# Loading token blocks 12 to 15 in two halves and moving one key transpose (kt12) forward, in a one-core transformer layer

## The chip, the core and the metric

The kernel runs on one core of a Trainium2 chip. The core has five engines that run their own instruction streams and meet through semaphores: TensorE (PE; its weight loads are listed apart as PEld), VectorE (DVE), ScalarE (ACT), GpSimd (POOL) and SyncE (SP), which here does nothing but issue DMAs, one after another, in the order of its program. SBUF is the on-chip memory, PSUM holds the results of matmuls in 8 banks. The metric is the device time of one execution in microseconds (us); smaller is better.

## The reference

One pre-norm layer on x of 2048 tokens by 640 features, in bf16: a memory-augmented attention over 4 segments of 512 tokens (32 heads of 20 features), then a dense part with 1728 hidden features. Cut to what matters:

```python
q = (x @ wq) ...; k = (x @ wk) ...; v = (x @ wv) ...      # x is layernorm(A_x); heads of 20, 4 segments
phi = lambda t: jnp.where(t > 0, t + 1.0, jnp.exp(t))
for s in range(N):                                         # 4 segments in order
    logits = einsum('bhqd,bhkd->bhqk', qs, ks) * scale + mask
    a_dot = einsum('bhqk,bhkd->bhqd', softmax(logits), vs)
    pq = phi(qs)
    a_mem = einsum(pq, M) / (einsum(pq, z) + 1e-06)
    outs.append(g * a_mem + (1.0 - g) * a_dot)
    pk = phi(ks)
    M = M + einsum('bhld,bhle->bhde', pk, vs)
    z = z + einsum('bhld->bhd', pk)
...
h = x + attention(layernorm(x)) @ wo
h2 = h + silu(layernorm(h) @ w1) @ w2
```

## The kernel before

**Tiling.** A token block is 128 tokens on the 128 partitions, so there are 16 blocks, four to a segment. x_tok holds 12 blocks; blocks 12 to 15 use the places of blocks 0 to 3 again, once their results are stored. All weights stay in SBUF.

**Steps and their names.** The work is cut into tasks, and each task has a name that says step, segment and index:

- x12 loads token blocks from memory (line 578). `load_x(12, 4, ...)` loads four blocks, 12 to 15, in one DMA of 640 KB.
- n1_st, n1_r, n1_ap and n1_tr with a block's number are the first layer norm: statistics on DVE (line 742), the reciprocal root on POOL (lines 760 and 763), the normalisation on DVE into xn_rot (line 769), and a DMA transpose from SP into xT (line 798). n2_ with the same letters is the second layer norm; its transposes go into hT, by the same line 798.
- pr are the query and key projections on PE (line 866), qe their evacuation from PSUM; v are the value projections (line 827). pr220, the first key or query projection of segment 2, reads xT of all four blocks 8 to 11.
- vt copies parts of q and k within SBUF into QKV (line 914, twelve small DMAs in a segment); vp does this for phi(q) into phiQv (line 927).
- qk are attention scores on PE (line 964), e their exponentials on ACT (line 976), mk the causal masks on POOL (line 987), av the products with v (line 1008), tn and nm the transposition, the memory term and the division (lines 1038, 1042, 1056 to 1062), ad their sum (line 1070). The first five head groups of a segment read QK, the last three read QKV. qk13a0 belongs to group 5 of segment 1 and so is the first that needs that segment's QKV.
- phb is the last step of phi (line 902 for keys and queries alike). kt with a segment and an index is the DMA transpose of phi(k) of one chunk of heads (line 1207), kg and kh gather parts of it (line 1198), mz is the product phi(k)·v on PE (line 1225), ma adds it to the memory (line 1241), mb masks it (line 1249). kt12 is segment 1, chunk 2; mz10 needs kt12 and kt13.
- ot and wo are the transposes of the attention's output (line 1264) and its projection (line 1272), rs the first residual (line 1280).
- h1, th and s are the hidden layer: matmul on PE (line 1307), tanh on ACT (line 1316), their product on DVE (line 1322), which frees the PSUM bank. h2 is the second matmul (line 1349), o the second residual (line 1362), out the store of a block (line 1367).

**Order.** The order of all tasks is written out by hand in one long table, ORDER. Every engine runs its share of the table in that order. The name after a slash is the engine (S for SP, A for ACT, G for POOL, D for DVE), the numbers after a colon are the slots (PSUM banks, buffers) that the task takes. The semaphore waits are derived from what tasks read and write. So a DMA that waits on SP holds everything behind it on SP. The stores of a segment's four blocks share one counter; a load that uses their places again waits for those stores that stand ahead of it in the table.

**Interleaving.** The segments overlap: the dense part of one segment runs in PE's stream between the attention of the next.

Of the kernel before, what the change touches and what calls it, by code (L numbers as in the profile page):

```python
# [234 lines left out]
class Graph:  # L235
# [51 lines left out]
    def schedule(self):  # L287
# [37 lines left out]
D = 640  # L325
# [23 lines left out]
P = {"ln1": -5.0, "ln1s": 0.524, "v": -2.2, "vs": 0.4, "pr": -0.979, "prc": 0.831, "prw": 0.404, "phq": 0.3,  # L349
# [37 lines left out]
qk10a0:0 e10a+:4 w_w2_4 s0_9_0 n1_tr8:0 h1_0_13_0:7 th0_13_0:1 pha101:0 h2_0_0:4 h2_0_1 mm2 ma02/D:7,2,6,3 pha130:0  # L387
phb100 ot2 qk10b0:0 mk8b_384 n1_ap9:2 av8:6 n1_tr10 mzc2 pha110:0 mzc4 s0_13_0 pha131:1 vt12/S w_w2_5 ex131:1 mk9b_0
mk9b_384 e10b+:6 mk9a_0 av9:7 phb131 kt13:0 vt13/S mzc1 oe9/D:1 vt17/S ex130:1 mzc6 pha111:2 oe8/D:0 phb101 vt11/S
h2_0_2 ex110:0 vt18/S n1_tr9 qk10e0:0 e10e2:0 n1_tr11 mk10b_0 vt15/S mk10b_384 h2_0_3 e10e0 mk10e_0 ex121:2 h2_1_0:6  # L390
o0 qk11a0:2 e11a+:3 phb130 pha121:1 phb121 kt12:1 vt14/S wo3:0 phb110 rs3 n2_st3:2 h2_1_1 qk11b0:2 mb00:0,0 ex140:2
n2_r3/G tn8:0 nm8:1,1 phb140 vp111/S:0 e11b+:1 mk10e_256 vp14/S h2_1_2 h2_1_3 o1 qk12a0:2 mk10a_0 vp10/S wo2:0 rs2
av10:6 vp13/S mk11a_0 vp110/S vp16/A e12a+:5 n2_ap3:2 ex141:1 mk11b_0 qk12b0:2 mz10:0 mb01:0,0 e12b0:2 pr220:7
oe10/D:0 ma10 e12b2 qk13a0:0 kg12/G:0 mk12a_0 mk11b_384 qe220/D:0 tn9:4 nm9:2,0 ad9:0 v20:6 e13a+:4 n2_tr3 kh13/G
# [13 lines left out]
rs6 n2_st6:3 ex220:2 av16:0 oe16/D:1 wo7:6 rs7 n2_r6/D qk17a0:2 wo4:0 vt28/S e17a+:0 h1_0_9_1:7 th0_9_1:0 ex240:1  # L408
kg10/G vt27/S n2_st7:0 mk18b_384 vt21/S mk17b_384 vt211/S h1_0_3_1:6 mk17a_0 rs4 th0_3_1:1 n2_st4:2 s0_9_1 qk18e0:2
e18e0:1 n2_r4/D wo5:0 s0_3_1 vt23/S h1_0_2_1:7 e18e2 mk18e_0 phb240 rs5 th0_2_1:0 s0_2_1 h1_0_1_1:6 th0_1_1:1 vt24/S  # L410
s0_1_1 qk18a0:2 e18a0:2 vt25/S av17:1 oe17/A:0 kt23:1 h2_2_0:6 h2_2_1 n2_ap6:1 n2_st5:6 n2_tr6:0 n2_r7/G mk18e_256
n2_ap7:3 n2_tr7 phb220 vt22/S e18a2 qk19b0:0 pha230:0 phb230 vp21/S:0 e19b0:4 tn17:4 nm17:3,1 n2_ap4:1 n2_tr4 pha200:0
h2_2_2 e19b2 h2_2_3 mk18a_0 n2_r5/G qk19a0:0 h2_3_0:4 h2_3_1 e19a2:0 o2 ad17:0 vp22/S e19a0 n2_ap5:3 n2_tr5 out2/S
mk19a_0 vp24/S ex200:0 kh14/D av18:6 oe18/D:0 vt210/A phb200 qk20b0:0 e20b+:3 h2_3_2 mk19b_0 h2_3_3 o3 vp25/S ex201:1
kg14/G mz12:7 mb10:0,0 tn18:1 nm18:3,0 mk19b_384 av19:0 h1_1_10_0:6 oe19/A:0 phb201 qk21b0:0 th1_10_0:1 tn16:4 ma12
s1_10_0:0 nm16:0,1 e21b+:4 mk21b_0 mk21b_384 h1_1_7_0:7 h1_1_4_0:6 ad18 th1_7_0:1 th1_4_0:0 s1_7_0 s1_4_0 qk20a0:0
e20a+:2 out3/S x12/S n1_st12:6 n1_r12/G h1_1_1_0:4 th1_1_0:1 s1_1_0 vp210/S h1_1_12_0:7 th1_12_0:0 mk20b_0 n1_st13:0
n1_r13/G mk20b_384 vp28/S qk20e0:0 h1_1_11_0:5 n1_ap12:3 e20e+:0 h1_1_8_0:4 qk21a0:0 s1_12_0 th1_11_0:1 h1_1_5_0:6
e21a+:5 th1_5_0:0 n1_st15:5 mk21a_0 n1_ap13:2 mk20a_0 s1_11_0 s1_5_0 mk20e_0 mk20e_256 h1_1_2_0:7 th1_2_0:1 s1_2_0
# [43 lines left out]
def build(nc, es, A_x, A_wq, A_wk, A_wv, A_wo, A_beta, B_x, B_w1, B_w2, out):  # L463
# [10 lines left out]
    G = Graph(pools)  # L474
# [100 lines left out]
    def load_x(b0, n, prio, bw=2.1, kind="plain", engs=(SP, AC)):  # L575
        s0 = b0 % 12
        dma(f"x{b0}", [], [(X[b], [0]) for b in range(b0, b0 + n)],
            lambda e: e.dma_start(out=x_tok[:, s0:s0 + n, :], in_=xv[:, b0:b0 + n, :]), prio, bw, kind, engs=engs)
# [846 lines left out]
```

## Time and profile before

| | us |
|---|---|
| three runs | 297.81, 298.67, 298.39 |
| median | 298.39 |
| the profiled execution | 298.91 |
| its span in the trace | 297.1 |
| PE busy in the span | 285.1 (96%) |
| DVE busy | 223.2 (75%) |
| ACT busy | 217.6 (73%) |
| POOL busy | 141.1 (48%) |

The table says that PE is busy nearly all of the span. A busy share is an average over the whole span, however, and tells nothing of single waits; these are read from the chain of waits (the work that ended last, followed back from the end), from the timeline of each engine, where idle time ahead of a row stands in brackets with what ended it, and from the DMA view, which gives the time from a DMA's issue to its landing. Times in these views count from the start of the span. A row of SPq or ACTq is the issue of a DMA, not its transfer.

### The profile page before, as it was taken

Reading aid. Unit: us, or ns where it says so; the run is one execution under the profiler, and the core shown is the slowest. Engines: PE = TensorE matmul, PEld = TensorE weight load, DVE = VectorE, ACT = ScalarE, POOL = GpSimd, SP = SyncE. Lnnn points to the kernel's source line nnn. Section 1 sums busy time; section 2 is a strip of 40 time slices with the busy share of each in tenths; the row PEclk is TensorE's granted clock in tenths of the full one; section 3 lists DMA queues with packets and bytes.
Section 4 is the critical chain, followed back from the end, with each engine's and each line's share of the span. In section 5 each row is a group of like instructions: output and inputs, shape, how many; then the busy total and the mean of one; then the engine's idle time right before and its main releaser. Section 6 shows DMA issues by size and latency. Waiting matters only on the chain.

```text
span 297.1 us, 7435 instructions
## 1 busy us (share of the span) xinstructions
PE 285.1 (96%) x2989; PEld 167.8 (56%) x2989; DVE 223.2 (75%) x503; ACT 217.6 (73%) x263; POOL 141.1 (48%) x261
## 2 busy tenths in 40 slices
PE   8898889999998999999998999999999999999996
PEld 5675445556664456566643444455665457764575
DVE  5897988868887979899678967759967688626522
ACT  5857997999997999999788999788759751013400
POOL 6226964665446776646525656354576630200000
PEclk9999999999999999999999999999999999999999
DMA  7946773924473422153343400154071023230002
GB/s 232 369 124 99 175 132 99 254 73 125 82 87 64 60 67 38 29 107 73 66 141 65 82 4 2 26 80 84 16 105 32 0 56 78 67 68 24 23 22 90
DMA packets 49906, 25.40 MB, mean 85 GB/s; under 512 B 39488, under 2 KB 48032, under 8 KB 49872
## 3 DMA queue, kind: packets, MB, share of 16 engines
q1 hardware_dynamic: 47656, 22.55, 35.9%
q10 hardware_dynamic: 2216, 2.38, 2.6%
q8 instruction: 24, 0.39, 0.6%
q14 instruction: 10, 0.08, 0.1%
HBM read 10.41 MB, written 2.62 MB: 44 GB/s over the span
## 4 chain that ended last, share of the span: by engine, by line
PE 73%; DVE 8%; ACT 7%; DMA 7%; issue 1%; POOL 1%; ACTq 1%; SPq 1%; DVEq 0%
PE ps_all L1349 18%; PE ps_all L1307 15%; PE ps_all L866 10%; PE ps_all L1272 7%; PE ps_all L827 6%; ACT PT L976 6%; PE ps_all L964 6%; PE ps_all L1008 5%; DMA x_tok<-in_A_x_dram 4%; DMA phiKt<-phiK 2%; DVE stt L742 2%; PE ps_all L1038 1%; PE ps_all L1225 1%; PE ps_all L1042 1%; PE ps_all L1301 1%
## 5 line engine op out<-in xcount | busy, mean ns | idle before, releaser
L976 ACT ACTIVATE PT<-ps_all 128x1024 bf16<-128x1024 f32 (+1 forms) x118 | 152.9, 1328 | 19.9 <-PE ps_all L964 16.4
L987 POOL TENSOR_SCALAR_AFFINE_SELECT PT<-PT 128x512 bf16<-128x512 bf16 x128 | 81.8, 651 | 50.7 <-ACT PT L976 49.0
L1349 PE MATMUL ps_all<-w_sb,sT 128*128 128x320 bf16 (+2 forms) x462 | 64.9, 295 | 0.1
L1307 PE MATMUL ps_all<-hT,w_sb 128*128 128x512 bf16 (+1 forms) x325 | 62.8, 337 | 1.3 <-DVE sT L1322 1.2
L1316 ACT ACTIVATE th<-ps_all 128x512 f32<-128x512 f32 (+2 forms) x70 | 33.9, 503 | 35.1 <-PE ps_all L1307 30.5
L1349 PEld LDWEIGHTS ps_all<-w_sb,sT 128*128 128x128 bf16 x462 | 43.2, 98 | 18.4 <-issue 2.0
L1322 DVE SCALAR_TENSOR_TENSOR sT<-th,ps_all 128x512 bf16<-128x512 f32 (+2 forms) x70 | 37.9, 561 | 18.7 <-ACT th L1316 17.9
L1307 PEld LDWEIGHTS ps_all<-hT,w_sb 128*128 128x128 bf16 x325 | 29.8, 98 | 26.7 <-issue 3.4
L763 POOL TENSOR_TENSOR rst<-rst,eps_c 128x1 f32<-128x1 f32 x32 | 18.6, 584 | 27.6 <-DVE rst L757 26.2
L742 DVE BATCH_NORM_STATS2 stt<-x_tok 128x6 f32<-128x320 bf16 x62 | 27.2, 482 | 2.7 <-DMA x_tok<-in_A_x_dram 2.2
L1362 DVE SCALAR_TENSOR_TENSOR x_tok<-ps_all,x_tok 128x640 bf16<-128x640 f32 (+3 forms) x18 | 13.3, 744 | 17.1 <-PE ps_all L1349 17.1
L1070 POOL TENSOR_TENSOR otok<-on 128x320 bf16<-128x320 bf16 x24 | 19.2, 802 | 13.8 <-DVE on L1062 13.8
L1272 PE MATMUL ps_all<-wo_sb,oT 128*128 128x320 bf16 x160 | 23.7, 299 | 0.0
L883 DVE CAST QK<-ps_all 128x512 bf16<-128x512 f32 x25 | 17.2, 687 | 5.9 <-PE ps_all L866 5.8
L1062 DVE TENSOR_TENSOR on<-ps_all,rd 128x640 bf16<-128x640 f32 x24 | 19.8, 824 | 0.9
L1272 PEld LDWEIGHTS ps_all<-wo_sb,oT 128*128 128x128 bf16 x160 | 15.0, 98 | 7.2 <-issue 1.8
L866 PE MATMUL ps_all<-xT,wkr 128*128 128x512 bf16 x75 | 18.7, 380 | 0.0
L827 PE MATMUL ps_all<-wv_sb,xT 128*128 128x320 bf16 x120 | 18.3, 299 | 0.4
L866 PE MATMUL ps_all<-xT,wqr 128*128 128x512 bf16 x75 | 18.2, 380 | 0.0
L1008 PE MATMUL ps_all<-PT,Vx 128*32 128x512 bf16 (+3 forms) x384 | 16.4, 301 | 0.0
L769 DVE TENSOR_SCALAR xn_rot<-x_tok,mvt,rst 128x640 bf16<-128x640 bf16 x32 | 14.7, 470 | 1.4 <-POOL rst L763 1.2
L889 ACT ACTIVATE ex<-QK 128x512 bf16<-128x512 bf16 x25 | 15.5, 630 | 0.1
(106 smaller groups left out, 336.2 us busy)
## 6 DMA issues: line engine op xcount, KB each, us to landing
w_sb<-in_B_w_dram SPq DMA_DIRECT2D x5, 432.0 KB, 3.6
x_tok<-in_A_x_dram SPq DMA_DIRECT2D x3, 640.0 KB, 8.7
w_sb<-in_B_w_dram SPq DMA_DIRECT2D x3, 480.0 KB, 3.6
out_dram<-x_tok ACTq DMA_DIRECT2D x9, 160.0 KB, 1.8
out_dram<-x_tok SPq DMA_DIRECT2D x6, 160.0 KB, 2.0
QKV<-QK SPq DMA_DIRECT2D x12, 72.0 KB
wo_sb<-in_A_wo_dram SPq DMA_DIRECT2D x1, 800.0 KB, 10.6
w_sb<-in_B_w_dram SPq DMA_DIRECT2D x1, 640.0 KB, 5.3
```

Source lines behind the costliest of these rows:

```text
L742: T.add(DV, lambda e, hh=hh: e.bn_stats(out=stt[:, s, 6 * hh:6 * hh + 6], in_=xb[:, 320 * hh:320 * hh + 320]), reads=R((xa, xsub)), writes ...
L827: fns.append(lambda e, c=c, hh=hh: e.matmul(bank(ps, hh)[:, 0:320], lhsT=xT_[:, c, 128 * i:128 * i + 128], rhs=wv_sb[:, c, 320 * hh:320 * ...
L866: fns = [lambda e, kc=kc: e.matmul(bank(ps)[:, lo:hi], lhsT=wt[:, kc, c, :], rhs=xT_[:, kc, lo:hi], start=(kc == 0), stop=(kc == NC - 1)) ...
L976: T.add(AC, lambda e: e.activation(out=pt[:, pta.slot, q0:q0 + nq, 0:width], in_=sc3[:, b0:b0 + nq, 0:width], func=ACT.Exp, scale=SCALE), ...
L987: T.add(PO, lambda e: e.affine_select(out=v, in_=v, pattern=[[0, 4], [1, 128]], compare_op=ALU.is_ge, fill=0.0, base=0, channel_multiplier ...
L1008: fns.append(lambda e, j=j, r=r, h=h, pa=pa, pt=pt, co=co, q0=q0, ji=ji: e.matmul(bank(po)[32 * r:32 * r + 32, q0:hi], lhsT=Vx[:, vx.slot, ...
L1062: T.add(DV, lambda e: e.tensor_tensor(out=on[:, ona.slot, :, :].rearrange("p b (x e) -> p b x e", e=DH), in0=v[:, :, :, 0:DH], in1=r2.unsq ...
L1272: fns.append(lambda e, c=c, hh=hh: e.matmul(bank(ps, hh)[:, 0:320], lhsT=oT[:, c, 128 * i:128 * i + 128], rhs=wo_sb[:, c, 320 * hh:320 * h ...
L1307: fns = [lambda e, c=c: e.matmul(bank(ps)[:, lo:hi], lhsT=w1_sb[:, c, 128 * f:128 * f + 128], rhs=hT[:, c, lo:hi], start=(c == 0), stop=(c ...
L1316: T.add(AC, lambda e: e.activation(out=th[:, tha.slot, lo:hi], in_=bank(ps)[:, lo:hi], func=ACT.Tanh, scale=0.5), reads=R((ps, [0])), writ ...
L1322: T.add(DV, lambda e: e.scalar_tensor_tensor(out=sT[:, f, lo:hi], in0=th[:, tha.slot, lo:hi], scalar=1.0, in1=bank(ps)[:, lo:hi], op0=ALU. ...
L1349: fns.append(lambda e, f=f, t0=t0, fr=fr, hh=hh, n=n: e.matmul(bank(pa, hh)[:, 0:n], lhsT=sT[:, f, t0:t0 + 128], rhs=w2_sb[:, fr, c0 + 320 ...
```

## The change

Two things change. First, `load_x(12, 4, ...)` becomes two loads of two blocks (320 KB each), x12 and x14. x14 stands in the table where x12 stood, behind out3, the store of block 3; x12 now stands behind kt23. Second, kt12 stands ahead of n1_tr9 and n1_tr11 in place of behind n1_tr9, n1_tr11 and vt15. No arithmetic changes.

```diff
@@ ORDER @@
-h2_0_2 ex110:0 vt18/S n1_tr9 qk10e0:0 e10e2:0 n1_tr11 mk10b_0 vt15/S mk10b_384 h2_0_3 e10e0 mk10e_0 ex121:2 h2_1_0:6
-o0 qk11a0:2 e11a+:3 phb130 pha121:1 phb121 kt12:1 vt14/S wo3:0 phb110 rs3 n2_st3:2 h2_1_1 qk11b0:2 mb00:0,0 ex140:2
+h2_0_2 ex110:0 vt18/S qk10e0:0 e10e2:0 mk10b_0 mk10b_384 h2_0_3 e10e0 mk10e_0 ex121:2 h2_1_0:6 o0 qk11a0:2 e11a+:3
+phb130 pha121:1 phb121 kt12:1 n1_tr9 n1_tr11 vt15/S vt14/S wo3:0 phb110 rs3 n2_st3:2 h2_1_1 qk11b0:2 mb00:0,0 ex140:2
...
-s0_1_1 qk18a0:2 e18a0:2 vt25/S av17:1 oe17/A:0 kt23:1 h2_2_0:6 h2_2_1 n2_ap6:1 n2_st5:6 n2_tr6:0 n2_r7/G mk18e_256
+s0_1_1 qk18a0:2 e18a0:2 vt25/S av17:1 oe17/A:0 kt23:1 x12/S h2_2_0:6 h2_2_1 n2_ap6:1 n2_st5:6 n2_tr6:0 n2_r7/G
...
-e20a+:2 out3/S x12/S n1_st12:6 n1_r12/G h1_1_1_0:4 th1_1_0:1 s1_1_0 vp210/S h1_1_12_0:7 th1_12_0:0 mk20b_0 n1_st13:0
+qk20a0:0 e20a+:2 out3/S x14/S n1_st12:6 n1_r12/G h1_1_1_0:4 th1_1_0:1 s1_1_0 vp210/S h1_1_12_0:7 th1_12_0:0 mk20b_0
...
@@ build @@
         if s == NSEG - 1:
-            load_x(12, 4, 8 * s + P["x3"])
+            load_x(12, 2, 8 * s + P["x3"])
+            load_x(14, 2, 8 * s + P["x3"])
```

What moves is SP's stream. The first place is in segment 1, with the QKV copies of that segment around it; phiKt<-phiK is kt12, the two transposes into xT are n1_tr9 and n1_tr11, and the copies are vt17, vt11 and vt18 at the top, vt15 in the middle, vt14 at the bottom. What an instruction waits for stands in brackets.

```order
 L914 DMA QKV<-QK 8x2x1024 x2
 L914 DMA QKV<-QK 8x1x1024
+L1207 DMA_TRANSPOSE phiKt<-phiK 128x4x128 [waits s_dve]
 L798 DMA_TRANSPOSE xT<-xn_rot 128x5x128 x2
 L914 DMA QKV<-QK 8x1x1024
-L1207 DMA_TRANSPOSE phiKt<-phiK 128x4x128 [waits s_dve]
 L914 DMA QKV<-QK 8x2x1024
```

kt12, with its wait for DVE, moved past two transposes and a copy.

The second place is later on SP, in the tail of segment 1: phiKt<-phiK is kt23, the transposes into hT are those of blocks 6 and 7.

```order
 L914 DMA QKV<-QK 8x1x1024
 L1207 DMA_TRANSPOSE phiKt<-phiK 128x4x128 [waits s_pool,s_dve]
+L578 DMA x_tok<-in_A_x_dram 128x2x640 [waits l_out0]
 L798 DMA_TRANSPOSE hT<-xn_rot 128x5x128 [waits s_pe,s_dve]
 L798 DMA_TRANSPOSE hT<-xn_rot 128x5x128 [waits s_dve]
```

A load of two blocks is new here; it waits for the stores out0 and out1. Further on, behind out3, the load of four blocks has become one of two:

```order
 L1367 DMA out_dram<-x_tok 128x640 [waits s_dve]
-L578 DMA x_tok<-in_A_x_dram 128x4x640 [waits l_out0]
+L578 DMA x_tok<-in_A_x_dram 128x2x640 [waits l_out0]
 L927 DMA phiQv<-phiQ 8x1024
 L927 DMA phiQv<-phiQ 8x1x512
```

It waits for all four stores, as before. On DVE one wait is new: the statistics of block 15, the first reader of x14, wait for it. PE, ACT and POOL run the same instructions in the same order.

More of the change, by code (lines that the diff above doesn't have):

```diff
@@ L410 @@
 e18e0:1 n2_r4/D wo5:0 s0_3_1 vt23/S h1_0_2_1:7 e18e2 mk18e_0 phb240 rs5 th0_2_1:0 s0_2_1 h1_0_1_1:6 th0_1_1:1 vt24/S
-s0_1_1 qk18a0:2 e18a0:2 vt25/S av17:1 oe17/A:0 kt23:1 h2_2_0:6 h2_2_1 n2_ap6:1 n2_st5:6 n2_tr6:0 n2_r7/G mk18e_256
-n2_ap7:3 n2_tr7 phb220 vt22/S e18a2 qk19b0:0 pha230:0 phb230 vp21/S:0 e19b0:4 tn17:4 nm17:3,1 n2_ap4:1 n2_tr4 pha200:0
-h2_2_2 e19b2 h2_2_3 mk18a_0 n2_r5/G qk19a0:0 h2_3_0:4 h2_3_1 e19a2:0 o2 ad17:0 vp22/S e19a0 n2_ap5:3 n2_tr5 out2/S
-mk19a_0 vp24/S ex200:0 kh14/D av18:6 oe18/D:0 vt210/A phb200 qk20b0:0 e20b+:3 h2_3_2 mk19b_0 h2_3_3 o3 vp25/S ex201:1
@@ L415 @@
-kg14/G mz12:7 mb10:0,0 tn18:1 nm18:3,0 mk19b_384 av19:0 h1_1_10_0:6 oe19/A:0 phb201 qk21b0:0 th1_10_0:1 tn16:4 ma12
-s1_10_0:0 nm16:0,1 e21b+:4 mk21b_0 mk21b_384 h1_1_7_0:7 h1_1_4_0:6 ad18 th1_7_0:1 th1_4_0:0 s1_7_0 s1_4_0 qk20a0:0
-e20a+:2 out3/S x12/S n1_st12:6 n1_r12/G h1_1_1_0:4 th1_1_0:1 s1_1_0 vp210/S h1_1_12_0:7 th1_12_0:0 mk20b_0 n1_st13:0
-n1_r13/G mk20b_384 vp28/S qk20e0:0 h1_1_11_0:5 n1_ap12:3 e20e+:0 h1_1_8_0:4 qk21a0:0 s1_12_0 th1_11_0:1 h1_1_5_0:6
-e21a+:5 th1_5_0:0 n1_st15:5 mk21a_0 n1_ap13:2 mk20a_0 s1_11_0 s1_5_0 mk20e_0 mk20e_256 h1_1_2_0:7 th1_2_0:1 s1_2_0
@@ L420 @@
-vp20/S qk22a0:0 e22a0:6 kt20:0 vp211/S kg20/G:0 n1_st14:4 vp26/S th1_8_0:1 kg23/D n1_r14/D h1_1_6_0:5 th1_6_0:0 vp29/S
-n1_tr12:0 v30:6 n1_r15/D s1_6_0 e22a2 h1_1_0_0:0 n1_ap14:0 s1_8_0 n1_ap15:3 mk22a_0 kh23/G av21:1 ve30/A:1
+s0_1_1 qk18a0:2 e18a0:2 vt25/S av17:1 oe17/A:0 kt23:1 x12/S h2_2_0:6 h2_2_1 n2_ap6:1 n2_st5:6 n2_tr6:0 n2_r7/G
+mk18e_256 n2_ap7:3 n2_tr7 phb220 vt22/S e18a2 qk19b0:0 pha230:0 phb230 vp21/S:0 e19b0:4 tn17:4 nm17:3,1 n2_ap4:1
+n2_tr4 pha200:0 h2_2_2 e19b2 h2_2_3 mk18a_0 n2_r5/G qk19a0:0 h2_3_0:4 h2_3_1 e19a2:0 o2 ad17:0 vp22/S e19a0 n2_ap5:3
@@ new lines @@
+n2_tr5 out2/S mk19a_0 vp24/S ex200:0 kh14/D av18:6 oe18/D:0 vt210/A phb200 qk20b0:0 e20b+:3 h2_3_2 mk19b_0 h2_3_3 o3
+vp25/S ex201:1 kg14/G mz12:7 mb10:0,0 tn18:1 nm18:3,0 mk19b_384 av19:0 h1_1_10_0:6 oe19/A:0 phb201 qk21b0:0 th1_10_0:1
+tn16:4 ma12 s1_10_0:0 nm16:0,1 e21b+:4 mk21b_0 mk21b_384 h1_1_7_0:7 h1_1_4_0:6 ad18 th1_7_0:1 th1_4_0:0 s1_7_0 s1_4_0
+qk20a0:0 e20a+:2 out3/S x14/S n1_st12:6 n1_r12/G h1_1_1_0:4 th1_1_0:1 s1_1_0 vp210/S h1_1_12_0:7 th1_12_0:0 mk20b_0
+n1_st13:0 n1_r13/G mk20b_384 vp28/S qk20e0:0 h1_1_11_0:5 n1_ap12:3 e20e+:0 h1_1_8_0:4 qk21a0:0 s1_12_0 th1_11_0:1
@@ L422 @@
+h1_1_5_0:6 e21a+:5 th1_5_0:0 n1_st15:5 mk21a_0 n1_ap13:2 mk20a_0 s1_11_0 s1_5_0 mk20e_0 mk20e_256 h1_1_2_0:7 th1_2_0:1
+s1_2_0 vp20/S qk22a0:0 e22a0:6 kt20:0 vp211/S kg20/G:0 n1_st14:4 vp26/S th1_8_0:1 kg23/D n1_r14/D h1_1_6_0:5 th1_6_0:0
+vp29/S n1_tr12:0 v30:6 n1_r15/D s1_6_0 e22a2 h1_1_0_0:0 n1_ap14:0 s1_8_0 n1_ap15:3 mk22a_0 kh23/G av21:1 ve30/A:1
 mb12:0,0,0,0 av20:2 qk22b0:3 vp23/S th1_0_0:0 s1_0_0 n1_tr13 mz20:7 ma20 oe21/A:1 e22b+:1 mk22b_0 vp27/S tn21:0
```

## The prediction, made before the changed kernel was run

> **What bounds the kernel now.** I read the chain of waits first, over its whole length. Apart from the start it is TensorE (PE) work, one matmul group behind another, and outside that it holds few stretches in which a DMA sets the pace. Two of them concern what the diff touches. Columns: start in us, length in us, what.
>
> ```profile
> 91.27 2.43 DMA phiKt<-phiK
> ...
> 149.77 2.44 DMA out_dram<-x_tok
> 152.22 4.76 DMA x_tok<-in_A_x_dram
> 157.01 0.90 DVE stt L742 x2
> ```
>
> The first is kt12, which lands at 93.70; mz10, the product that needs it, starts then. The second is three long: store of block 3, load of blocks 12 to 15, and the statistics of block 12 (L742) that wait for it. Next the table of busy time by stretch (length, then busy time of PE, PEld, DVE, ACT, POOL, granted clock, DMA share, GB/s), to see whether time won at one place lasts.
>
> ```profile
> 94.00:120.00 26.00, 25.88 (x307) 14.08 (x303) 21.18 (x45) 23.70 (x28) 18.74 (x32) 1.00 0.28 50
> 175.00:200.00 25.00, 24.99 (x266) 12.56 (x265) 16.68 (x32) 21.58 (x25) 13.13 (x21) 1.00 0.22 31
> ```
>
> PE is busy 25.88 of 26.00 and 24.99 of 25.00 us at full clock, with ACT next. So behind both places the kernel runs on PE's sequence, and a microsecond that PE gains there should move everything behind it, as long as no SP transfer stands at a fixed time.
>
> **First part: kt12 ahead.** The engines' timelines around it; the bracket is idle time and what ended it.
>
> ```profile
> 85.85 0.64 DVE L902 TENSOR_TENSOR phiK<-phiK,ex 128x512 bf16<-128x512 bf16 x1
> 87.14 3.38 SPq L798 DMA_TRANSPOSE xT<-xn_rot  x2
> 90.56 0.66 SPq L914 DMA_DIRECT2D QKV<-QK  x1
> 92.51 0.72 SPq L914 DMA_DIRECT2D QKV<-QK  x1
> 92.54 0.40 PE L964 MATMUL ps_all<-QK 20*128 20x384 bf16 x8
> 93.75 0.47 PE L1225 MATMUL ps_all<-Vx,phiKt 128*128 128x84 bf16 x8 [0.81 <-DMA phiKt<-phiK]
> 94.06 1.24 PE L866 MATMUL ps_all<-xT,wqr 128*128 128x512 bf16 x5
> 95.24 0.39 PE L964 MATMUL ps_all<-QKV 20*128 20x512 bf16 x4
> ```
>
> SP issues without a pause here. kt12's own input (phb121, DVE L902) is ready at 85.85 + 0.64 = 86.49, but SP gets to it at 91.27, behind the two xT transposes and one QKV copy. In the changed order SP reaches kt12 at 87.14, after 86.49, so its wait for DVE costs SP nothing, and nothing that stands behind it is held for that reason. PE is free at 92.54 + 0.40 = 92.94; kt12 then has 5.8 us to land where the chain shows 2.43. The 0.81 us before mz10 go.
>
> What is late next? The two xT transposes n1_tr9 and n1_tr11 and one QKV copy (vt15) each go one kt12 later. The instructions are the same, so SP is back in step for the next QKV copy, vt14, at 92.51. The group behind mz10, pr220 (L866), needs xT of all four blocks, and PE would want it at 92.94 + 0.47 = 93.41. Time from issue to landing of n1_tr9, of n1_tr11, and of an xT transpose of segment 3 that follows no other transpose closely:
>
> ```profile
> xT<-xn_rot SPq DMA_TRANSPOSE x1, 4.2
> xT<-xn_rot SPq DMA_TRANSPOSE x1, 3.7
> xT<-xn_rot SPq DMA_TRANSPOSE x1, 2.6
> ```
>
> In their new place the two take SP from 87.14 + 1.24 = 88.4 to 91.75, if they need their 3.38 again (one of them was hindered: two hT transposes further on take 2.55, so 1.25 to 1.3 is the plain issue). If the last issue is plain, n1_tr11 begins at 91.75 - 1.25 = 90.5 and lands between 90.5 + 2.6 = 93.1 and 90.5 + 3.7 = 94.2. The first end is in time for 93.41; the last gives back all of the 0.81. If it is the hindered one, it begins earlier, at 89.6, and lands by 89.6 + 4.2 = 93.8. I take the first, the row of a transpose of the same size on a free queue, since the hindrance fell before 90.5.
>
> Behind pr220 PE has qk13a0 (95.24), the first matmul on the QKV copies of this segment; it needs all of them, vt14 last. That copy keeps its issue at 92.51. No row gives its landing; the table by quarter microseconds bounds it:
>
> ```profile
> 94.75:95.00 0.25, 0.25 (x3) 0.06 (x1) 0.00 (x0) 0.18 (x1) 0.25 (x1) 1.00 0.03 8
> 95.00:95.25 0.25, 0.25 (x6) 0.02 (x4) 0.00 (x0) 0.00 (x0) 0.25 (x1) 1.00 0.00 0
> ```
>
> DMA data (last column) runs out by 95.0, and 92.51 plus kt12's own 2.43 is 94.94. PE would be there at 95.24 - 0.81 = 94.43. So the QKV copy probably takes over as the wait, and qk13a0 starts near 94.95, which is 0.29 earlier than before. Some of the rest comes back at once, because the next PE groups do not need the copies but the evacuation of pr220, which is 0.8 earlier. Bounds of the first part: 0 (nothing, or a few hundredths lost) to 0.81 won; between 0.29 and 0.81 I take 0.4, nearer to the copy.
>
> **Second part: the load in halves.** The later half, x14, stays where the whole load stood, behind the store of block 3. The first half, x12, goes behind kt23.
>
> ```profile
> 128.78 0.59 SPq L1367 DMA_DIRECT2D out_dram<-x_tok  x1
> ...
> 135.48 1.23 SPq L1207 DMA_TRANSPOSE phiKt<-phiK  x1
> 138.05 2.55 SPq L798 DMA_TRANSPOSE hT<-xn_rot  x2
> ...
> 152.22 0.41 SPq L578 DMA_DIRECT2D x_tok<-in_A_x_dram  x1
> ```
>
> x12 waits only for the stores of blocks 0 and 1. The second of these is issued at 128.78 and by the 2.44 of block 3's store lands at 131.2, so the wait is over when SP comes to it at 135.48 + 1.23 = 136.71. Its issue (0.41 for the whole load) fits before 138.05, when DVE releases the next transpose: it costs SP nothing. If that cover were gone, 0.4 us of SP would be added. It lands before 136.71 + 4.76 = 141.5, the time of a load twice its size, 13 us ahead of need.
>
> ```profile
> 155.71 1.09 ACT L1316 ACTIVATE th<-ps_all 128x512 f32<-128x512 f32 x2
> 156.66 1.91 ACT L976 ACTIVATE PT<-ps_all 128x2048 bf16<-128x2048 f32 x1
> 153.44 1.33 DVE L1322 SCALAR_TENSOR_TENSOR sT<-th,ps_all 128x512 bf16<-128x512 f32 x2 [0.22 <-ACT th L1316]
> 157.01 0.89 DVE L742 BATCH_NORM_STATS2 stt<-x_tok 128x6 f32<-128x320 bf16 x2 [2.23 <-DMA x_tok<-in_A_x_dram]
> 160.55 0.88 DVE L742 BATCH_NORM_STATS2 stt<-x_tok 128x6 f32<-128x320 bf16 x2
> 156.28 1.25 PE L1307 MATMUL ps_all<-hT,w_sb 128*128 128x512 bf16 x5
> 158.75 1.25 PE L1307 MATMUL ps_all<-hT,w_sb 128*128 128x512 bf16 x5 [1.22 <-DVE sT L1322]
> 159.93 0.40 PE L964 MATMUL ps_all<-QKV 20*128 20x512 bf16 x4
> ```
>
> DVE stands 2.23 us for the load. Queued behind it is the s step (L1322) that frees the PSUM bank PE wants at 157.53; PE stands 1.22 for that. With x12 there, DVE does the statistics at 154.8. The s step then waits only for its tanh on ACT, the first of the pair that begins at 155.71, so it ends near 156.9, before PE asks. PE's 1.22 go. Not 2.23: two groups on, PE's scores (159.93) need the banks that ACT's exponential frees at 156.66 + 1.91 = 158.57, so PE cannot gain more than 159.93 - 158.6 = 1.33. I take 1.2, the idle time itself.
>
> x14 is issued at 152.22 as before and needs at most the whole load's 4.76: 157.0. Its first reader, the statistics of block 15, came 160.55 - 157.01 = 3.5 us behind those of block 12, so now at 154.8 + 3.5 = 158.3. Hidden by 1.3 us.
>
> **Sum.** 0.4 + 1.2 = 1.6 us. The profiled execution took 298.91, of which 297.1 are the span and 1.8 lie around it: 295.5 and 297.3. The median of the runs lies 0.52 below the profiled one, so 298.39 - 1.6 = 296.8.
>
> **The rivals.** *The first part gives nothing*: the xT transpose of block 11 lands at 94.2, not 93.1, and PE starts pr220 when it did before. For it: in the old order it took 3.7. Against it: a transpose behind a quiet queue took 2.6. Only 1.2 remain: 297.2.
>
> *The second wait is replaced*: everything comes earlier by DVE's order, but ACT, which works through 155.71 to 158.57 without a gap, keeps PE waiting for scores, and half of the 1.2 goes. With 0.4 from the first part: 1.0 gained at most, or 0.6 if the xT transpose is late too, so 297.4 to 297.8. If the early half is for some reason held by its wait until the old place, only the first 0.4 is left: 298.0.
>
> *Slower*: the early half is put ahead of the four hT transposes of segment 1, and stretches them. The copy ahead of their later two, these two, and PE's first group on them:
>
> ```profile
> 141.37 0.66 SPq L927 DMA_DIRECT2D phiQv<-phiQ  x1
> 142.40 2.56 SPq L798 DMA_TRANSPOSE hT<-xn_rot  x1
> 145.71 1.97 SPq L798 DMA_TRANSPOSE hT<-xn_rot  x1
> ...
> hT<-xn_rot SPq DMA_TRANSPOSE x1, 3.4
> 149.27 1.25 PE L1307 MATMUL ps_all<-hT,w_sb 128*128 128x512 bf16 x5
> ```
>
> The last lands at 145.71 + 3.4 = 149.1, and PE uses it at 149.27: almost no slack. An issue took 2.56 instead of 2.55 / 2 = 1.28 when it was hindered. Should x12's data hinder the two transposes at 138.05 so, SP would be 2 x 1.28 = 2.6 behind, less the 0.4 that it idles before 142.40: the last would land at 151.3. PE, 0.4 early at 148.9, would wait 2.4, and after the 1.2 won later the kernel would be 2.4 - 1.6 = 0.8 slower: 299.2, more if the later two are hindered further. It decides once SP is over 1.4 us behind at 142.40 (0.2 + 1.4 = the 1.6 won). Against it: x12 is over by 141.5, and DVE, not SP, released 138.05.
>
> The Trainium skill bears on this rival (DMA: Bandwidth & Descriptors, section Queues, rings and completion order): on each DMA engine the descriptors of one ring are consumed in the order of the ring, so the transposes behind x12 begin their data after it. By that alone the transpose at 138.05 is moved to 141.5 at the latest and the one at 145.71 not at all, so by the rule this case would be far less likely than I make it. The trace agrees only in part: the transposes of 4.2 and 3.7 stand behind a row of copies, but the one at 142.40, hindered too, stands behind a small one (141.37).
>
> **How the numbers follow.** Both parts as summed: 0.50 (own range 296.2 to 297.2, from 2.14 and 1.2 won). First part nothing: 0.20. Second replaced or held: 0.17. Slower: 0.13. No change here means within 0.3%, 0.9 us, about what a measurement of this kernel can tell. Faster by more needs under 297.5: the first two cases and a little of the third less the edges, 0.70. Same 0.17, slower 0.13. The range, 295.8 to 298.3, takes in the first three cases and leaves out the slower one and some scatter of the runs (0.86 us between the three shown).
>
> **What would show it.** The 0.81 before L1225 at 93.75 and the 2.23 before L742 are gone from the waits; pr220 does not wait for xT; the QKV matmul behind it waits a few tenths for a copy; x14's reader does not wait; PE is 0.4 early at 100 and 1.6 early from 165 to the end. It is wrong if the first L1307 group near 149 waits for an hT transpose, or if the lead at 165 is not there at 250.

## The result, and the profile after

The changed kernel took 297.28 us (median of 19 runs, 296.56 to 298.40), the kernel before in the same comparison 298.47 us (19 runs, 297.44 to 299.66). The ratio is 0.9962, 95% interval [0.9948, 0.9976], which is 1.13 us won (0.7 to 1.55 by the interval). The profiled execution took 297.49, of which 295.8 are the span.

**First place.** The timeline of SP in the changed kernel (start, length, what):

```profile
87.18 1.20 SPq L1207 DMA_TRANSPOSE phiKt<-phiK  x1
88.42 3.25 SPq L798 DMA_TRANSPOSE xT<-xn_rot  x2
91.71 1.40 SPq L914 DMA_DIRECT2D QKV<-QK  x2
```

kt12 now goes out 4.09 us earlier than before (91.27). In its new place it lands after 4.2 us instead of 2.43, at 91.3 and still in time. But the five instructions take as long as in the old order: the last QKV copy, vt14, ends at 91.71 + 1.40 = 93.11, where it ended at 92.51 + 0.72 = 93.23. PE shows who is late next:

```profile
92.28 0.40 PE L964 MATMUL ps_all<-QK 20*128 20x384 bf16 x8
92.69 0.46 PE L1225 MATMUL ps_all<-Vx,phiKt 128*128 128x84 bf16 x8
93.40 1.02 PE L866 MATMUL ps_all<-xT,wqr 128*128 128x512 bf16 x4 [0.25 <-issue]
94.89 0.40 PE L964 MATMUL ps_all<-QKV 20*128 20x512 bf16 x4 [0.46 <-DMA QKV<-QK]
...
97.27 0.29 PE L964 MATMUL ps_all<-QK 20*128 20x256 bf16 x4 [0.21 <-ACT PT L976]
```

The 0.81 in front of mz10 (L1225) are gone. In their place qk13a0 waits 0.46 for the QKV copy, and 2.4 us on PE waits 0.21 for ACT's exponentials, which started with qk13a0. The 0.25 "<-issue" before L866 is no wait: the group has 5 matmuls and one record is missing (x4, 1.02 us; before x5, 1.24). The same goes for the x9 and its 0.16 below.

**Second place.** The timelines of DVE, ACT and PE in the changed kernel:

```profile
153.09 1.33 DVE L1322 SCALAR_TENSOR_TENSOR sT<-th,ps_all 128x512 bf16<-128x512 f32 x2 [0.22 <-ACT th L1316]
154.34 0.88 DVE L742 BATCH_NORM_STATS2 stt<-x_tok 128x6 f32<-128x320 bf16 x2
155.99 0.69 DVE L1322 SCALAR_TENSOR_TENSOR sT<-th,ps_all 128x512 bf16<-128x512 f32 x1 [0.53 <-ACT th L1316]
...
155.35 1.09 ACT L1316 ACTIVATE th<-ps_all 128x512 f32<-128x512 f32 x2
156.30 1.91 ACT L976 ACTIVATE PT<-ps_all 128x2048 bf16<-128x2048 f32 x1
...
156.15 2.11 PE L1307 MATMUL ps_all<-hT,w_sb 128*128 128x512 bf16 x9 [0.16 <-issue]
158.27 0.39 PE L964 MATMUL ps_all<-QKV 20*128 20x512 bf16 x4
```

The DMA view, x12 and then x14 (size, us from issue to landing):

```profile
x_tok<-in_A_x_dram SPq DMA_DIRECT2D x1, 320.0 KB, 3.4
x_tok<-in_A_x_dram SPq DMA_DIRECT2D x1, 320.0 KB, 2.9
```

DVE's 2.23 for the load and PE's 1.22 behind it are gone. The s step waits for its tanh and ends at 156.68 (156.9 was predicted). The scores, at 159.93 before, stand at 158.27, just after ACT's exponential ends at 156.30 + 1.91 = 158.21: PE now runs as close behind ACT here as it can.

**Where the time went.** To add up such places over several runs, I take the start of the same PE instruction in two traces. The table gives it minus its start in the profiled execution of before (us, minus is earlier). The columns are the instruction's start in before: 92.54 is the group ahead of mz10, 95.24 is qk13a0, 105 a score group ten us on, 146 a point ahead of the second place, 159.93 the scores behind it, 260 late in the dense part.

| kernel | 92.54 | 95.24 | 105 | 146 | 159.93 | 260 |
|---|---|---|---|---|---|---|
| the change | -0.27 | -0.34 | -0.36 | -0.36 | -1.66 | -1.66 |
| the change again (e6) | +0.01 | -0.53 | -0.54 | -0.54 | -1.85 | -1.71 |
| kt12 alone (e1) | +0.15 | -0.29 | -0.31 | -0.32 | -0.71 | -0.53 |
| kt12 alone again (e11) | +0.01 | +0.34 | +0.32 | +0.32 | -0.48 | -0.33 |
| halves alone (e2) | -0.22 | -0.99 | -1.00 | -1.00 | -2.31 | -2.20 |
| halves alone again (e7) | +1.09 | +1.11 | +1.11 | +1.12 | -0.18 | -0.19 |
| halves, both late (e3) | -0.32 | -0.30 | -0.29 | -0.30 | -1.60 | -1.60 |

The first column is the chance of the execution (PE has met no wait that the change touches by then): it is spread from -0.32 to +1.09. What a part is worth is the difference between columns. From 146 to 159.93 the change gains 1.30; from 92.54 to 105 it gains 0.09. Both stay to 260. The other 0.27 of the 1.66 was there before the first place was reached.

### The profile page after: what moved, and what is told of

The parts are those of the page before. It is cut to its first block, busy times and chain, and to the rows that moved or that the text cites. A ratio compares the mean times of both kernels' runs of the same rounds, so it can differ in the third digit from the quotient of the medians.

```text
span 295.8 us, 7413 instructions
## 1 busy us (share of the span) xinstructions
PE 282.3 (95%) x2966; PEld 168.1 (57%) x2989; DVE 223.0 (75%) x503; ACT 217.3 (73%) x263; POOL 141.2 (48%) x261
## 4 chain that ended last, share of the span: by engine, by line
PE 76%; ACT 8%; DVE 6%; DMA 3%; issue 2%; SPq 1%; POOL 1%; ACTq 1%
PE ps_all L1349 18%; PE ps_all L1307 17%; PE ps_all L866 11%; ACT PT L976 7%; PE ps_all L964 7%; PE ps_all L1272 6%; PE ps_all L827 6%; PE ps_all L1008 5%; PE ps_all L1038 2%; DVE stt L742 1%; SPq L798 1%; DMA phiKt<-phiK 1%; PE ps_all L1042 1%; DMA x_tok<-in_A_x_dram 1%; PE ps_all L1301 1%
## 5 line engine op out<-in xcount | busy, mean ns | idle before, releaser
L1307 PE MATMUL ps_all<-hT,w_sb 128*128 128x512 bf16 (+1 forms) x315 | 60.8, 336 | 1.2 <-issue 0.6
L866 PE MATMUL ps_all<-xT,wkr 128*128 128x512 bf16 x68 | 17.2, 380 | 0.9 <-issue 0.6
L866 PE MATMUL ps_all<-xT,wqr 128*128 128x512 bf16 x69 | 17.1, 380 | 0.6 <-issue 0.4
```

The source lines that it names most:

```text
L866: fns = [lambda e, kc=kc: e.matmul(bank(ps)[:, lo:hi], lhsT=wt[:, kc, c, :], rhs=xT_[:, kc, lo:hi], start=(kc == 0), stop=(kc == NC - 1)) ...
L1307: fns = [lambda e, c=c: e.matmul(bank(ps)[:, lo:hi], lhsT=w1_sb[:, c, 128 * f:128 * f + 128], rhs=hT[:, c, lo:hi], start=(c == 0), stop=(c ...
```

## The experiments

Three readings of the first part stood against one another, by the letters of the expectations: A, the copies into QKV behind mz10 swallow what kt12 wins; B, the first part is worth the predicted 0.4; C, formed after the first four runs, the 0.81 is no fixed cost but the mark of one execution, because issue and landing of the DMA transposes differ from execution to execution. Where an expectation words a letter itself, that holds. The second part (halves) had one question: is it the size of the load, or its early place?

**The two parts apart.** e1 is before with kt12 moved and nothing else, e2 before with the load in halves and nothing else; their diffs are the two parts of the change. e11 and e7 time the same two again, and e6 the change itself.

> Only kt12 is moved; blocks 12 to 15 come in one late load as before. Theory A (the QKV copy vt14 takes over as the wait): mz10 starts 0.7 to 0.8 us earlier, the first QKV matmul behind it waits some 0.3 to 0.5 us for a copy and starts 0.1 to 0.35 us earlier than in the kernel before, and the whole gains 0 to 0.35 us: 298.1 to 298.5 against 298.47. The 2.2 us wait of the statistics of block 12 for the load stays. Theory B (the move brings its full 0.8 us): 297.7.

> Only the load is split, its first half issued behind kt23; kt12 stands where it stood. Theory A (the load carries nearly all of the change): the wait of 0.8 us for kt12 stays, the wait for the load goes, PE is 1.2 to 1.3 us earlier behind the place and stays so: 297.2. Theory B (both parts carry about the half of it, and together 1.2): 297.9.

| | median us | ratio to before | interval |
|---|---|---|---|
| e1, kt12 alone | 298.28 | 1.0010 | [0.9987, 1.0032] |
| e11, the same | 298.04 | 1.0007 | [0.9982, 1.0033] |
| e2, halves alone | 297.54 | 0.9973 | [0.9951, 0.9995] |
| e7, the same | 297.41 | 0.9985 | [0.9964, 1.0005] |
| e6, the change again | 296.97 | 0.9961 | [0.9941, 0.9981] |

(Before took 297.89 in e1's and e2's comparison, 298.06 in e6's and e7's, 298.04 in e11's. A ratio is the comparison's own figure and not the quotient of the two medians; for e2 that quotient would be 0.9988.) Alone, kt12 gains nothing that can be measured, in either comparison; the halves alone gain in one, and in the other their interval just reaches 1. The median of e2 lies between the 297.2 of its A and the 297.9 of its B and decides for neither. In the trace of e1, the wait of qk13a0 for the copy is 0.29 and its start 0.30 earlier than in before, close to what A had. DVE and PE of the second place stand as in before, only shorter:

```profile
94.94 0.40 PE L964 MATMUL ps_all<-QKV 20*128 20x512 bf16 x4 [0.29 <-DMA QKV<-QK]
...
156.29 0.89 DVE L742 BATCH_NORM_STATS2 stt<-x_tok 128x6 f32<-128x320 bf16 x2 [1.83 <-DMA x_tok<-in_A_x_dram]
...
158.03 1.25 PE L1307 MATMUL ps_all<-hT,w_sb 128*128 128x512 bf16 x5 [0.82 <-DVE sT L1322]
```

e2 brought the surprise. kt12 stands in its old place, and still PE does not wait for it (SP, then PE):

```profile
86.98 2.56 SPq L798 DMA_TRANSPOSE xT<-xn_rot  x2
89.59 0.66 SPq L914 DMA_DIRECT2D QKV<-QK  x1
90.30 1.19 SPq L1207 DMA_TRANSPOSE phiKt<-phiK  x1
...
92.76 0.47 PE L1225 MATMUL ps_all<-Vx,phiKt 128*128 128x84 bf16 x8
```

The pair of xT transposes took 2.56 us to issue where it took 3.38 in before, and kt12 went out 0.97 earlier. So the wait that the first part removes was not there in this execution.

> The changed kernel as it is, timed again beside e7 on the same chip. The theories agree on the second part: PE 1.3 us earlier at 160 than at 150. On the first part, theory A expects qk13a0 to wait about 0.5 us for the QKV copy again and PE to be no more than 0.1 us earlier behind it than ahead of 87 us; theory C (issue and landing of the DMA transposes differ from execution to execution) allows the wait to be gone if n1_tr9 and n1_tr11 take 1.3 us each to issue. Time: about 1.2 us below before, 0.996.

> The load in halves alone, kt12 in its old place, timed again beside the changed kernel. Theory A (the first part is worth 0 to 0.1 us): no difference from the changed kernel beyond 0.3 us, ratio to before 0.996 to 0.997; PE 1.3 us earlier at 160 than at 150. Theory C: the wait of mz10 for kt12 is 0.8 us when the xT transposes in front of it are hindered (landing over 3.5 us) and gone when they are not (landing under 3 us). Theory B (the first part is worth its 0.4): the changed kernel is 0.4 us faster than this one.

e7 has the same program as e2, its pair takes 2.71, and kt12 is waited for again:

```profile
94.86 0.47 PE L1225 MATMUL ps_all<-Vx,phiKt 128*128 128x84 bf16 x8 [0.83 <-DMA phiKt<-phiK]
```

e3, whose kt12 also stands in its old place (below), has the wait too:

```profile
93.45 0.47 PE L1225 MATMUL ps_all<-Vx,phiKt 128*128 128x84 bf16 x8 [0.83 <-DMA phiKt<-phiK]
```

In e6 qk13a0 waits only 0.20 for the copy, and PE gains 0.55 at the first place where A allowed 0.1. Both have the 1.3 of the second place (table above: 1.31 and 1.30). C's numbers hold in e7 only roughly: the first transpose landed after 3.46, under the 3.5 that C named for a hindered one. What made e7 late stands ahead of the pair. SP began the key transpose kt13 0.71 later than in before, and kt13 and the four copies behind it took 1.1 us longer:

```profile
83.51 1.86 SPq L1207 DMA_TRANSPOSE phiKt<-phiK  x1
85.41 3.48 SPq L914 DMA_DIRECT2D QKV<-QK  x4
```

So SP was 1.80 late when it came to the pair (88.94 against 87.14), PE only 1.09 late at the group ahead of mz10. By the times, the change and the halves alone differ by 0.24% in this comparison, in favour of the change, with intervals that overlap; kt12 alone against before points the other way.

> kt12 ahead alone, the load whole and late, timed again. Theory A: PE gains 0 to 0.4 between 87 and 99 us (the three executions with kt12 ahead so far: 0.05 lost, 0.42 and 0.32 gained), with the wait of qk13a0 for the QKV copy where it gains little; DVE stands about 2 us for the load and PE over 1 us behind it, as before. Ratio 0.999 to 1.000. Theory B (worth its 0.4 or more): ratio 0.9985 or less. Rival (it costs something that the trace of one execution does not show): ratio over 1.001 again.

In e11 the pair behind kt12 took 3.75 to issue, and now the xT transpose was late:

```profile
88.60 3.75 SPq L798 DMA_TRANSPOSE xT<-xn_rot  x2
...
93.87 1.24 PE L866 MATMUL ps_all<-xT,wqr 128*128 128x512 bf16 x5 [0.44 <-DMA xT<-xn_rot]
95.57 0.40 PE L964 MATMUL ps_all<-QKV 20*128 20x512 bf16 x4 [0.47 <-issue]
...
158.26 1.25 PE L1307 MATMUL ps_all<-hT,w_sb 128*128 128x512 bf16 x5 [0.41 <-DVE sT L1322]
```

PE lost 0.31 at the first place instead of gaining: outside what A allowed (0 to 0.4 gained). For the 0.47 ahead of qk13a0 the profile names no releaser; the late QKV copy is the likely one. The 0.44 ahead of L866 is the wait of the prediction's rival "the first part gives nothing".

**Is it the early place or the size of the load?** e3 leaves kt12 in its old place and issues both halves behind out3, where the whole load stood.

```diff
-e20a+:2 out3/S x12/S n1_st12:6 n1_r12/G
+e20a+:2 out3/S x12/S x14/S n1_st12:6 n1_r12/G
...
-            load_x(12, 4, 8 * s + P["x3"])
+            load_x(12, 2, 8 * s + P["x3"])
+            load_x(14, 2, 8 * s + P["x3"])
```

> The load is split, but both halves are issued one behind the other at the late place, behind out3; kt12 stands where it stood. Theory C (it is the landing of the first two blocks that counts, and a half lands in 2.9 to 3.4 us in place of 4.8): the statistics of block 12 wait at most 0.8 us instead of 2.2, the tanh on ACT is then what the s step waits for, and 0.9 to 1.3 us are won: 297.2 to 297.6. Theory D (only the early issue helps; two halves issued together share the queue and the first lands about as late as the whole): 298.1 to 298.5.

Median 297.65, ratio 0.9981 [0.9959, 1.0002]. The timelines of SP, DVE and PE:

```profile
150.14 0.92 SPq L578 DMA_DIRECT2D x_tok<-in_A_x_dram  x2
...
154.40 0.88 DVE L742 BATCH_NORM_STATS2 stt<-x_tok 128x6 f32<-128x320 bf16 x2
...
158.33 0.39 PE L964 MATMUL ps_all<-QKV 20*128 20x512 bf16 x4
```

The DMA view has x12's landing, and that of the whole load in e1, which was issued at the same 150.14:

```profile
x_tok<-in_A_x_dram SPq DMA_DIRECT2D x1, 320.0 KB, 3.2
```

```profile
x_tok<-in_A_x_dram SPq DMA_DIRECT2D x1, 640.0 KB, 6.1
```

x12 lands at 150.14 + 3.2 = 153.3, ahead of the statistics at 154.40, and the full 1.30 is gained. The early place is not needed: what counts is that the statistics of block 12 no longer wait for the data of blocks 14 and 15. The whole load lands after 6.1 us in e1, 5.7 in e11, 6.5 in e5 and 4.8 in before. One thing favours e3: before issued its load only at 152.22, since two hT transposes ahead of it took 2.56 and 1.97 us to issue (1.20 and 1.23 in e3) and the store that it waits for landed after 2.44 (1.77). A half issued then would land at 155.4 by e3's 3.2, and the s step behind the statistics would end near 157.1, still ahead of the 157.53 at which PE wants its bank; this is an estimate from the rows of before, and no run shows it.

**Is it the QKV copy that swallows the gain?** e4 is the change with one of the two remaining QKV copies, vt15, issued by ACT instead of SP; e10 is the same again, and e8 does it on the halves alone.

```diff
-phb130 pha121:1 phb121 kt12:1 n1_tr9 n1_tr11 vt15/S vt14/S wo3:0
+phb130 pha121:1 phb121 kt12:1 n1_tr9 n1_tr11 vt14/S wo3:0
...
-av10:6 vp13/S mk11a_0 vp110/S vp16/A e12a+:5
+av10:6 vp13/S mk11a_0 vp110/S vp16/A vt15/A e12a+:5
```

> The changed kernel, with the QKV copy vt15 issued by ACT behind vp16 in place of SP, so that vt14 is issued on SP 0.7 us earlier. Theory A (the QKV copy is what takes the gain of kt12): the wait of 0.46 us of the first QKV matmul for a copy goes, and 0.3 to 0.45 us more than in the changed kernel are won: 296.9 against 297.28. Theory E (the gain is lost further on anyway, to ACT's exponentials): the wait goes, but PE is no earlier at 100 us: 297.3.

e4's median is 297.91, ratio 0.9992 [0.9970, 1.0014]. Its trace bears A out: vt14 goes out at 90.99 instead of 92.42, and qk13a0 starts without a wait.

```profile
90.99 0.70 SPq L914 DMA_DIRECT2D QKV<-QK  x1
...
94.17 0.40 PE L964 MATMUL ps_all<-QKV 20*128 20x512 bf16 x4
```

PE gains 0.80 between 92.54 and 105 (-0.27 to -1.07) and loses 0.23 near 150. The times do not follow, so it was run again.

> The changed kernel with the QKV copy vt15 on ACT's queue, timed again beside e11. Theory A (the QKV copy swallowed the first part's gain): no wait of qk13a0 for the copy, PE 0.5 to 0.8 us earlier at 99 than at 87 against before, and 0.3 to 0.5 us less than the first part alone leaves there; with 0.2 lost at 150 the kernel is at 0.994 to 0.996 of before. Rival (it was no better than the changed kernel because the copy on ACT's queue costs as much as it saves): ratio 0.997 to 0.999 again and the loss to be seen somewhere in the trace behind 99.

Median 298.24, ratio 1.0002 [0.9980, 1.0024]: the ratio is outside what either reading gave (0.994 to 0.996, 0.997 to 0.999), though the interval takes in the second. The profiled execution shows one way to lose it all (SP, then PE):

```profile
88.58 4.65 SPq L798 DMA_TRANSPOSE xT<-xn_rot  x2
...
94.75 1.24 PE L866 MATMUL ps_all<-xT,wqr 128*128 128x512 bf16 x5 [1.44 <-DMA xT<-xn_rot]
```

The pair took 4.65 us, and PE lost 0.79 where e4 gained 0.80, with the same program.

> The load in halves, kt12 in its old place behind the two xT transposes, and the QKV copy vt15 issued by ACT in place of SP. SP loses 0.66 us of issue ahead of kt12 and vt14, so both are issued 0.66 us earlier without another order: kt12's wait falls from 0.81 to 0.15 us and the QKV copy is not waited for. Theory A: PE is 0.65 us earlier than before from 95 us on, besides the 1.3 us of the load from 160 on: 2.0 us in all, ratio 0.993 to 0.994, and better than the changed kernel by 0.6. If the copy on ACT's queue costs PE something (e4 lost 0.2 at 150), 0.2 less. Rival: the first place has no lasting worth at all, then the ratio is that of e7.

e8: 297.16, 0.9963 [0.9943, 0.9984]. PE gains 0.80 at the first place (+0.24 to -0.56; 0.65 was expected), without a wait at mz10 or qk13a0, loses 0.24 near 150 and gains 1.30 at the second: all as A has it. But by its time it is no better than the change. So of two programs with vt15 on ACT's queue, one is as good as the change and one is worse, and none is a better version.

**What is kt12's lateness worth?** e5 is before with kt12 behind vt14, one place later still.

```diff
-o0 qk11a0:2 e11a+:3 phb130 pha121:1 phb121 kt12:1 vt14/S wo3:0
+o0 qk11a0:2 e11a+:3 phb130 pha121:1 phb121 vt14/S kt12:1 wo3:0
```

> The kernel before, with kt12 one place later still: behind vt14, the last QKV copy. The first part of the change turned round, to see what kt12's lateness is worth. kt12 is issued 0.72 us later (vt14's issue), so mz10 should wait 0.81 + 0.72 = 1.5 us for it; qk13a0, which wants vt14, has that copy 1.2 us earlier and does not wait. Theory A (a delay at mz10 is passed on to all PE work behind it, and the QKV copy was the only thing that swallowed the gain): everything from mz10 on is 0.7 us later than in before, and so is the end: 0.7 over the median of before. Theory C (the 0.81 is not a fixed cost; it depends on how far the two xT transposes in front are hindered in the execution): the wait at mz10 comes out anywhere between 0 and 1.5, according to the landing time of n1_tr9, n1_tr11 and kt12 that this execution shows.

Median 298.81, ratio 1.0034 [1.0011, 1.0057], 1.0 us slower: A's 0.7 lies within it. The trace, though, shows no such loss at this place (PE +0.61 at 92.54, +0.58 at 105):

```profile
87.78 2.58 SPq L798 DMA_TRANSPOSE xT<-xn_rot  x2
...
94.32 0.48 PE L1225 MATMUL ps_all<-Vx,phiKt 128*128 128x84 bf16 x8 [0.78 <-DMA phiKt<-phiK]
```

The pair was issued in 2.58 instead of 3.38, 0.80 less, which pays for the 0.72 of vt14. In this execution the delay and the luck cancel. That the longer time of the 10 runs is kt12's delay is likely, but no trace shows it.

**Where would the early half do harm?** e9 is the change with x12 right ahead of the last hT transpose of segment 1.

```diff
-s0_1_1 qk18a0:2 e18a0:2 vt25/S av17:1 oe17/A:0 kt23:1 x12/S h2_2_0:6
+s0_1_1 qk18a0:2 e18a0:2 vt25/S av17:1 oe17/A:0 kt23:1 h2_2_0:6
...
-n2_tr5 out2/S mk19a_0 vp24/S ex200:0
+x12/S n2_tr5 out2/S mk19a_0 vp24/S ex200:0
```

> The changed kernel, with x12 moved from behind kt23 to right ahead of the last hT transpose of segment 1 (n2_tr5), the place where the prediction's slower rival would bite hardest. In the changed kernel that transpose is issued at 144.59, lands at 147.43, and PE takes its first group on it at 149.13, so there are 1.5 us to spare against PE's need of 148.97. SP idles from 144.10 to 144.59, so the issue of x12 itself (0.58) costs SP 0.1. Slower rival: the transpose is hindered by x12's data: its issue rises from 1.23 to about 2.5 and its landing from 2.84 to between 3.5 and 4.3 us, that is to 148.2 to 149.0, and PE waits 0 to 0.1; if it has to wait for all of x12's data (3.42 from issue: 147.5) and then take its own 2.84, it lands at 150.3 and PE waits 1.4, which gives back all of the second part. Theory of the second part (only the landing of blocks 12 and 13 before 154.8 counts): x12 lands near 147.5 to 148, PE gains 1.3 at 157 to 160 as in the changed kernel, time as that of the changed kernel.

Median 297.50, ratio 0.9981 [0.9956, 1.0006]. The timelines of SP and, for the first group on the transposes, PE:

```profile
144.77 0.50 SPq L578 DMA_DIRECT2D x_tok<-in_A_x_dram  x1
145.31 1.21 SPq L798 DMA_TRANSPOSE hT<-xn_rot  x1
...
149.55 1.24 PE L1307 MATMUL ps_all<-hT,w_sb 128*128 128x512 bf16 x5
```

From issue to landing of the two, in the DMA view:

```profile
x_tok<-in_A_x_dram SPq DMA_DIRECT2D x1, 320.0 KB, 4.0
hT<-xn_rot SPq DMA_TRANSPOSE x1, 4.1
```

The issue of the transpose is not stretched (1.21), its landing is: 4.1 instead of the changed kernel's 2.8 (3.3 to 3.6 in the other eleven executions), so it lands at 149.4, 0.7 after x12 (148.7) and 0.1 ahead of PE. Half a microsecond or more of harm is thus to be seen, and in the worst place it just fits; in the place of the change PE has 1.5 us to spare. PE gained 1.30 at 157 to 160 here too (+0.27 to -1.03). The Trainium skill (DMA: Bandwidth & Descriptors, section "Queues, rings and completion order") says that on each DMA engine a ring's descriptors are consumed in order; the landing order here agrees with it.

## Why the prediction was right, step by step

**The second part, 1.2 forecast, 1.30 found.** DVE's and PE's waits went, for the reason given, and the gain sits at the upper bound of 1.33, where ACT's exponential takes over, in every execution with halves. The s step, x14 (it lands at 153.0, and block 15 is read at 158.54) and SP came out as worked out, but for the issue of x12, which took 0.58 and not 0.41 and was covered all the same. What the prediction credited without need is the early place: e3 gains as much without it. And the 1.2 itself is one execution's: with the whole load PE waited 1.22 (before), 1.21 (e5), 0.82 (e1) and 0.41 (e11), 0.9 in the mean.

**The first part, 0.4 forecast, 0.09 found in the profiled execution.** The mechanism was right. kt12 went out at 87.18 (87.14 forecast) and was there in time. The QKV copy did take over, and qk13a0 started at 94.89 (94.95 forecast). The step that failed is the term's size, "between 0.29 and 0.81 I take 0.4, nearer to the copy". The rest did not come back behind qk13a0, because the scores after it wait 0.21 for exponentials that start only once qk13a0 is done. So no more than the copy's 0.35 (95.24 to 94.89; 0.29 forecast) could stay, and of that 0.27 were PE's already: by the chance of its start it came to this place early, and SP did not, since the key transpose kt13 took longer to issue. SP's row of the changed kernel, and of before:

```profile
82.24 1.87 SPq L1207 DMA_TRANSPOSE phiKt<-phiK  x1
```

```profile
82.80 1.26 SPq L1207 DMA_TRANSPOSE phiKt<-phiK  x1
```

0.56 early at the start of it, SP is 0.05 late at its end, and kt12 and the copies follow at the times of before.

**Beneath that: 0.81 was taken as a fixed cost, and the wait that replaces it as well.** From 92.54 to 105, PE gained in the executions with kt12 ahead and vt15 on SP 0.09 (the change), 0.55 (e6), 0.46 (e1), 0.46 (e9, +0.53 to +0.07) and lost 0.31 (e11), a mean of 0.25 gained. With kt12 in its old place and vt15 on SP it was 0 (before itself), 0.78 gained (e2), 0.02 lost (e7) and 0.03 lost (e3), a mean of 0.18 gained. The two means differ by 0.07 in favour of the new order. The single executions are spread so far that these nine can tell 0.07 neither from nothing nor from the predicted 0.4.

The wait of 0.8 at mz10 is no rarity: three of the four executions in the old order have it (0.81, 0.83, 0.83), and only e2 has none. But the new order pays as well, in all five: 0.20 to 0.47 at qk13a0, then 0.2 at the scores behind it, and in e11 0.44 at pr220 besides. How much is paid hangs on how late SP comes, and that differs from execution to execution, by the pair of xT transposes (2.56 to 3.75 us to issue) and by kt13 ahead of it (1.26 to 1.88). So A tells how the new order pays, and C why the gain scatters. But the 0.81 is not the mark of one execution, as C has it, and the two xT transposes to which e7's expectation ties it are too narrow a cause: in e7 SP was late before it came to them. B's 0.4 is not borne out by the mean and not excluded either. The times do not settle it. Without the halves the first part gains nothing (e1 and e11); with them it shows 0.24% (e6 against e7), within the intervals.

**The sum.** 0.07 and 0.9 make about 1.0, an estimate from these means and no surer than they are, beside the 1.13 measured and the 1.6 forecast. "PE is 0.4 early at 100 and 1.6 early from 165 to the end" reads as if fulfilled (0.36 and 1.66), but 0.27 of both is the chance of the two starts. At the very end the span is only 1.3 shorter, since the last store took 1.8 us to land and not 1.5.

**The rivals.** The 297.28 lies just above the 296.2 to 297.2 of the case that both parts come as summed. "The first part gives nothing" came nearest, and its 297.2 is nearest to the median too; its mechanism, the late xT transpose, was seen in e11 and e10, while in the changed kernel's own trace it is the QKV copy. "The second wait is replaced" did not happen in any run: ACT bounds the gain but only at 1.3. "Slower" did not happen; of the transposes behind x12 the second landed after 5.0 us (before 4.4), yet the last of the four was issued earlier than before and landed at 144.59 + 2.8 = 147.4. That before had 149.1 there, "almost no slack", was that execution's chance, with its two slow issues; without the early half it was 147.5 in e1 and e3. And e9 shows that even the worst place is within the slack.

## What to carry to other kernels

When a consumer reads a large load piece by piece, cut the load where the consumer first waits: the first piece then lands on its own, and here no earlier place in the queue was needed for that. Moving one transfer ahead of others in the same queue only pays by the distance to the next reader of that queue, so list who waits for each of the transfers that are overtaken, and expect the gain to end there. A wait for a DMA that one execution shows should be looked for in a second and third execution before it goes into a sum.

## What the runs showed of the hardware

In some executions the DMA engines move next to nothing for 1 to 2 us while the transposes are under way. The stretches of half a microsecond around the xT pair, of before, of e10 and of e2 (the last two columns are DMA share and GB/s):

```profile
88.50:89.00 0.50, 0.50 (x6) 0.38 (x4) 0.45 (x3) 0.50 (x1) 0.19 (x1) 1.00 3.52 191
89.00:89.50 0.50, 0.50 (x6) 0.35 (x5) 0.47 (x2) 0.50 (x1) 0.43 (x1) 1.00 0.77 9
89.50:90.00 0.50, 0.50 (x5) 0.25 (x3) 0.50 (x2) 0.27 (x1) 0.50 (x2) 1.00 0.08 9
```

```profile
89.00:89.50 0.50, 0.50 (x6) 0.35 (x5) 0.47 (x2) 0.50 (x1) 0.42 (x2) 1.00 3.78 173
89.50:90.00 0.50, 0.50 (x9) 0.20 (x6) 0.50 (x2) 0.03 (x1) 0.50 (x2) 1.00 0.00 0
...
91.00:91.50 0.50, 0.50 (x6) 0.39 (x4) 0.27 (x1) 0.50 (x1) 0.50 (x2) 1.00 0.00 0
```

```profile
89.00:89.50 0.50, 0.50 (x5) 0.36 (x4) 0.50 (x1) 0.50 (x1) 0.50 (x2) 1.00 0.48 66
89.50:90.00 0.50, 0.50 (x8) 0.20 (x5) 0.50 (x2) 0.06 (x1) 0.50 (x2) 1.00 0.79 162
```

The clock is full throughout. In before there are 9 GB/s from 89.0 to 90.0, in e10 0 to 9 from 89.5 to 91.5; each time the half microsecond ahead has a DMA share far over 1, which I read as packets that began there and hung. In e2 data flow on. The issue of the transpose that falls into the silence is long in step with it: the pair took 2.56 us in e2, 3.38 in before and 4.65 in e10. The silence comes in the old order and the new, with and without the copy on ACT's queue, and in two executions of one program once and once not (e4 2.77, e10 4.65). What causes it was not found, and no run was made to find it, so why e4 and e10 are slower than the change over 24 runs stays open too.

The size of the scatter was unexpected as well: PE's lead over before at 92.54 differs by 1.4 us between executions whose programs are the same up to there. The first of it arises at the start. The scores of segment 0 in before, and in e7:

```profile
12.04 0.40 PE L964 MATMUL ps_all<-w_sb 20*128 20x256 bf16 x12
```

```profile
12.82 0.34 PE L964 MATMUL ps_all<-w_sb 20*128 20x256 bf16 x8
```

0.78 of e7's 1.09 stand there after 12 us. This is why the two parts' gains are read inside a trace, from one column to the next, and not from its span.
